# Seven half products instead of eight in five groups of a Trainium2 attention and feed-forward kernel

## The chip, the cores and the metric

One core of one Trainium2 chip runs the kernel. The metric is the time of one execution on the device in microseconds, as a median of several runs. The engines named below are TensorE (PE; its weight loads are PEld), VectorE (DVE), ScalarE (ACT), GpSimd (POOL) and SyncE (SP, which here issues DMAs). Each has its own queue and works it off in order.

## The reference

Attention with normalised queries and keys, and then a gated feed-forward block on its output:

```python
batch, n_heads, seq, head_dim = (8, 12, 448, 64)
q_n, k_n = rmsnorm(q, g_q), rmsnorm(k, g_k)
scores = 1.0 / np.sqrt(64) * np.matmul(q_n, k_n.transpose(0, 1, 3, 2))
attn = np.exp(scores - np.max(scores, axis=-1, keepdims=True))
attn = attn / (np.sum(attn, axis=-1, keepdims=True) + 1e-09)
out = np.matmul(attn, v)
x = out.transpose(0, 2, 1, 3).reshape(8 * 448, 768)
g = x @ w_gate                    # 768 x 1536
val = x @ w_val                   # 768 x 1536
y = (g * (1.0 / (1.0 + np.exp(-g))) * val) @ w_out    # 1536 x 768
```

The attention inputs are float32, the three weights come as float64 and are turned into float32 by the kernel.

## The kernel before

The kernel takes the batches two at a time: four **blocks** of 2 x 448 tokens. Block n has an up phase (`w_gate` and `w_val`, silu and the product of the two), and then a down phase (`w_out`), into which the attention of the next block's 12 pairs of heads is woven. Attention of the first block stands ahead of everything, and the weights are converted beside it and in block 1.

The feed-forward products are made by a bilinear scheme: the two batches of a block and three row thirds of a weight give 6 pieces, a weight has 3 x 3 blocks, and 15 products (numbered 0 to 14) take the place of 18. `UP_ORDER` is the order of the 15. Their left sides, sums of weight blocks, are made once and lie in device memory (`up_sides`, `down_sides`); their right sides, sums of activations, lie in `xs`. `sides` makes them.

An up phase has four **groups** g (0 to 3) of 128 x 3 hidden units. In a group each of the 15 products is made twice, for `w_gate` (`which` 0, banks `mm0` and `mm1`) and for `w_val` (`which` 1, the two banks of `at`), each as two matmuls of 128 x 128 by 128 x 448 (`NC2` halves of the contraction). This is `up_product`, a function within `block`. Products of one chain add up in a PSUM bank, and after each one the bank is read: by ScalarE where the value is new (`COPY`), else by VectorE, which adds to or subtracts from an accumulator. When a result (one of 6 in a group) is complete for the gate, ScalarE applies silu into a PSUM tile `st` (two buffers), and VectorE weighs it by the value: `weigh`. The 24 results of a block lie in `gt`; `combine` makes of them the right sides of the 15 down products, in `hs`, `xs` and `gt`.

Weights come from device memory into two buffers `ws` by `up_load` and `load_sides`: a piece holds five of the 15 products, is issued by SP in two DMAs, and a buffer is free when its last product is done.

The order of instructions on each engine isn't written out. Every piece of work is put into an `Order` with an engine, an estimated duration, a due time (`when`), what it comes after and which buffers it takes or uses; `Order.run` plays this through and emits the pieces in the order that comes out. The due times come from `block_start`, `block_end` and `PRODUCT`, the time of an up product of one `which`.

Of the kernel before, what the change touches and what calls it, by code (L numbers as in the profile page):

```python
# [9 lines left out]
F32 = mybir.dt.float32  # L10
# [350 lines left out]
def transfer(rows, size):  # L361
    return rows * (6.64 + 0.045 * min(size, 4096)) / 16000.0
# [131 lines left out]
def fast(  # L494
# [41 lines left out]
    nc = tc.nc  # L536
# [31 lines left out]
        rr=4, ws=2, **{x + str(i): 1 for x in "vw" for i in range(6)},  # L568
# [14 lines left out]
    OFTEN = dict(w1=0, w2=1, w3=2, w4=3, rows=4)  # L583
# [49 lines left out]
    UP_SUMS = (8, 1, 7, 13, 10, 14, 3, 5, 11, 0, 4)  # L633
# [4 lines left out]
    down_sides = dram.tile([P, 2, NG, 15, P], F32, name="down_sides")  # L638

# [26 lines left out]
    UP, DOWN, BOTH = 30 * NG * PRODUCT, 90.7, 170.0  # L666
# [3 lines left out]

    def block_start(n):
        return FIRST + n * (UP + BOTH) + MORE * (n > 0)

    def block_end(n):
        return block_start(n) + UP + MORE * (n == 0)
# [722 lines left out]
    }  # L1398
    DOWN_READ = {
# [39 lines left out]
    def block(n):  # L1439
        add = order.add  # L1440
        start = block_start(n)
        unit = (block_end(n) - start) / (30 * NG)
# [10 lines left out]
        def up_product(g, step, x, which, load, key):  # L1453
            nonlocal last
            when = start + (2 * (15 * g + step) + which) * unit

            b = ("BCDAE".index(CHAIN[x]) % 2 if CHAIN[x] != "E" else 0) ^ (g % 2) ^ (n > 0)
# [111 lines left out]
        def up_load(g, piece):  # L1569
            key = ("ws", (n, g, piece))  # L1570
            load = add(
                "SP", 1.2, start + (30 * g + 10 * piece) * unit - 24.0,
# [7 lines left out]

        for g in range(NG):
            steps = [(step, which) for step in range(15) for which in range(2)]
            if n == 0 and g == 0:
                steps[: 2 * HEAD] = sorted(steps[: 2 * HEAD], key=lambda of: of[::-1])
            for step, which in steps:
                if step % 5 == 0 and which == 0:
                    key, load = up_load(g, step // 5)
                up_product(g, step, UP_ORDER[step], which, load, key)
        up_done[n] = last
        if n < NB - 1:  # L1590
# [3 lines left out]
            )  # L1594
        bank_read[:] = [free[0, 0], free[0, 1]]
# [32 lines left out]
        for g in range(NG):  # L1628
            when = start + 30 * (g + 1) * unit + 1.0
            before = [down_done.get(n - 1)] + ([staged[HS]] if n == 0 else [])  # L1630
# [8 lines left out]
        def down_product(step, x, s):  # L1639
# [18 lines left out]
            def emit():  # L1658
# [3 lines left out]
                for g in range(NG):  # L1662
                    nc.tensor.matmul(  # L1663
                        banks[s][:, 0:S], w[:, s, g, at], where[x][:, g],
# [6 lines left out]
                    last, loads[piece], bank_read[s], *made.get(x, []),  # L1671
# [10 lines left out]
            def emit_read():  # L1682
# [5 lines left out]
                read(how, tiles[value], old, banks[s][:, 0:S])  # L1688
# [6 lines left out]
            bank_read[s] = drained[s, t] = done  # L1695
# [167 lines left out]
```

## Time and profile before

| what | value |
|---|---|
| time, median of 3 runs | 1454.96 us (1453.89 to 1457.8) |
| span of the profiled execution, first to last instruction | 1452.0 us |
| its own time beyond the span | not recorded; the three runs lie 1.9 to 5.8 us above the span, the median 2.96 |
| mean granted TensorE clock | 0.997 |
| up phase of block 2 (n = 1) | 479.6 to 660.0 us |
| group 0 of block 3 (n = 2) | 826.9 to 872.0 us |
| groups 1 and 2 of block 3 | 872.0 to 962.2 us |
| group 0 of block 4 (n = 3) | 1173.8 to 1218.9 us |
| groups 1 to 3 of block 4 | 1218.9 to 1354.2 us |
| down phase of block 4 | 1354.2 to 1430 us |

The profile is one execution as the hardware profiler saw it. A row of a group of instructions gives line, engine, operation, tiles and shapes, count, busy time, the mean duration in ns, and the idle time of the engine ahead of them with what ended it. A row of the timeline gives start, duration and how many like instructions follow each other. A float32 matmul stands as two instructions, called passes below; a matmul's end is modelled, so consecutive ones overlap in the records and the distance of their starts is what counts.

### The profile page before, as it was taken

Reading aid. Unit: us, or ns where it says so; the run is one execution under the profiler, and the core shown is the slowest. Engines: PE = TensorE matmul, PEld = TensorE weight load, DVE = VectorE, ACT = ScalarE, POOL = GpSimd, SP = SyncE. Lnnn points to the kernel's source line nnn. Section 1 sums busy time; section 2 is a strip of 40 time slices with the busy share of each in tenths; the row PEclk is TensorE's granted clock in tenths of the full one; section 3 lists DMA queues with packets and bytes.
Section 4 is the critical chain, followed back from the end, with each engine's and each line's share of the span. In section 5 each row is a group of like instructions: output and inputs, shape, how many; then the busy total and the mean of one; then the engine's idle time right before and its main releaser. Section 6 shows DMA issues by size and latency. Waiting matters only on the chain.

```text
span 1452.0 us, 19362 instructions
## 1 busy us (share of the span) xinstructions
PE 1426.0 (98%) x6736; PEld 689.5 (47%) x6736; DVE 879.8 (61%) x1485; ACT 601.6 (41%) x1210; POOL 405.7 (28%) x476
## 2 busy tenths in 40 slices
PE   8999999999999999999999999999999999999997
PEld 4455454534444455544444455544444445555553
DVE  5889876878866434546877642455686644442533
ACT  6875444476653222356564122345555322212100
POOL 4756666625443000022443200011434300000000
PEclk9999999999999999999999999999999999999999
DMA  7778979854643533433644623443463452322235
GB/s 196 217 219 268 352 266 310 260 149 90 129 103 64 133 102 92 114 113 70 122 98 86 138 74 107 107 112 93 85 126 77 95 135 73 108 73 90 69 100 110
DMA packets 410416, 193.29 MB, mean 133 GB/s; under 512 B 280004, under 2 KB 390852, under 8 KB 410308
## 3 DMA queue, kind: packets, MB, share of 16 engines
q1 hardware_dynamic: 399040, 190.57, 49.1%
q10 hardware_dynamic: 11140, 1.38, 0.7%
q8 instruction: 55, 0.90, 0.3%
q14 instruction: 53, 0.43, 0.1%
q0 software_dynamic: 128, 0.00, 0.0%
HBM read 157.29 MB, written 34.60 MB: 132 GB/s over the span
## 4 chain that ended last, share of the span: by engine, by line
PE 90%; DMA 3%; DVE 2%; ACT 2%; SPq 1%; issue 1%; POOL 1%; ACTq 0%; DVEq 0%; POOLq 0%
PE at L1474 25%; PE mm L1474 25%; PE mm L1663 23%; PE at L1049 8%; PE st L970 7%; PE st L1080 1%; PE mm L1080 1%; DMA out_dram<-spare 1%; SPq L768 1%; DMA work<-in_k_dram 1%; ACT es L985 1%; DMA xs<-in_moe_w_gate_dram 0%; PE st L908 0%; DMA v<-in_v_dram 0%; ACT work L918 0%
## 5 line engine op out<-in xcount | busy, mean ns | idle before, releaser
L1474 PE MATMUL at<-xs,ws 128*128 128x448 f32 x960 | 401.2, 540 | 2.5 <-DVE v L1413 1.4
L1474 PE MATMUL mm<-xs,ws 128*128 128x448 f32 x960 | 401.7, 541 | 0.2 <-DVE hs L1315 0.2
L1474 PEld LDWEIGHTS at<-xs,ws 128*128 128x128 f32 x960 | 181.4, 190 | 184.7 <-issue 166.7
L1474 PEld LDWEIGHTS mm<-xs,ws 128*128 128x128 f32 x960 | 182.2, 190 | 180.7 <-issue 177.9
L888 POOL TENSOR_TENSOR work<-work,rr 128x448 f32<-128x448 f32 x72 | 71.8, 1016 | 467.5 <-DVE rr L715 341.6
L1663 PE MATMUL mm<-gt,ws 128*128 128x448 f32 x448 | 175.5, 543 | 0.0
L970 PE MATMUL st<-work 64*64 64x448 f32 (+1 forms) x1536 | 151.2, 501 | 10.3 <-ACT work L918 4.9
L985 ACT ACTIVATE es<-st 128x896 f32<-128x896 f32 x129 | 114.2, 914 | 101.6 <-PE at L1049 87.8
L1411 DVE TENSOR_TENSOR gt<-gt,mm 128x448 f32<-128x448 f32 x64 | 39.7, 621 | 188.1 <-PE mm L1474 161.7
L1663 PE MATMUL mm<-hs,ws 128*128 128x448 f32 x384 | 151.3, 544 | 0.0
L990 POOL TENSOR_TENSOR sums<-es 128x896 f32<-128x896 f32 x36 | 77.2, 2145 | 176.8 <-PE st L1080 83.7
L1663 PEld LDWEIGHTS mm<-gt,ws 128*128 128x128 f32 x448 | 83.6, 190 | 83.0 <-issue 80.8
L1551 ACT ACTIVATE st<-gt 128x448 f32<-128x448 f32 x96 | 52.3, 547 | 159.1 <-DVE gt L1415 85.7
L1409 ACT COPY gt<-mm 128x448 f32<-128x448 f32 x80 | 42.6, 532 | 157.5 <-PE mm L1474 157.4
L1049 PE MATMUL at<-es,v 64*64 64x448 f32 (+1 forms) x1032 | 106.0, 507 | 0.0
L1663 PEld LDWEIGHTS mm<-hs,ws 128*128 128x128 f32 x384 | 71.3, 190 | 71.0 <-issue 70.1
L970 PEld LDWEIGHTS st<-work 64*64 64x64 f32 x1536 | 50.9, 133 | 79.1 <-issue 37.4
L1409 ACT COPY v<-at 128x448 f32<-128x448 f32 x96 | 51.0, 532 | 80.4 <-PE at L1474 79.6
L990 POOL TENSOR_TENSOR sums<-sums,es 128x896 f32<-128x896 f32 x36 | 76.0, 2112 | 2.8
L1049 PEld LDWEIGHTS at<-es,v 64*64 64x64 f32 (+1 forms) x1032 | 44.1, 134 | 56.2 <-issue 50.4
L1554 DVE SCALAR_TENSOR_TENSOR gt<-st,v 128x448 f32<-128x448 f32 x96 | 59.7, 622 | 7.3 <-DVE v L1415 0.5
L1411 DVE TENSOR_TENSOR v<-v,at 128x448 f32<-128x448 f32 x64 | 39.8, 621 | 39.6 <-PE at L1474 39.5
(170 smaller groups left out, 1550.5 us busy)
## 6 DMA issues: line engine op xcount, KB each, us to landing
ws<-up_sides SPq DMA_DIRECT2D x32, 1024.0 KB, 5.6
ws<-down_sides SPq DMA_DIRECT2D x16, 1024.0 KB, 5.7
ws<-down_sides SPq DMA_DIRECT2D x28, 512.0 KB, 4.8
ws<-up_sides SPq DMA_DIRECT2D x16, 768.0 KB, 4.9
out_dram<-spare SPq DMA_DIRECT2D x168, 56.0 KB, 2.1
v<-in_v_dram SPq DMA_DIRECT2D x96, 96.0 KB, 2.5
ws<-up_sides SPq DMA_DIRECT2D x32, 256.0 KB, 5.9
ws<-up_sides SPq DMA_DIRECT2D x16, 512.0 KB, 5.8
```

What stands on the lines that cost most here:

```text
L888: nc.gpsimd.tensor_tensor(out=tiles["t", m][:, x], in0=tiles["qk", (m, x)], in1=rr.to_broadcast([P, NC, C]), op=ALU.mult,)
L970: nc.tensor.matmul(st[ds(D * x, D), h, 0:n], tiles["KT", m][rows, ds(P * j + D * of_keys, D)], tiles["QT", m][rows, ds(Q * of_queries, n)] ...
L985: nc.scalar.activation(e, tiles["st", (m, j)][:, :, 0 : S * width(j) // P], AF.Exp)
L990: nc.gpsimd.tensor_tensor(out=to, in0=tiles["e", (m, 0)] if j == 1 else to, in1=e, op=ALU.add)
L1049: nc.tensor.matmul(tiles["at", (m, x)][ds(D * h, D), ds(0, Q) if early else queries], tiles["v", m][rows, j, h], tiles["e", (m, j)][rows, ...
L1080: nc.tensor.matmul(to[ds(D * h + C * x, C)], halves[:, x] if half else many[:, 0:C], term[:, h, 0:Q] if half else term[:, h, ts(x, Q)], st ...
L1409: nc.scalar.copy(to, ps)
L1411: nc.vector.tensor_tensor(out=to, in0=old, in1=ps, op=ALU.add)
L1474: nc.tensor.matmul(ps(), w[:, which, c, at], xs[:, SLOT[x], c], start=fresh and c == 0, stop=c == NC2 - 1, skip_group_check=True,)
L1551: nc.scalar.activation(take(*act, [P, 2, TB])[:, 0, 0:S], to, AF.Silu)
L1554: nc.vector.scalar_tensor_tensor(to, tiles[act][:, 0, 0:S], 1.0 / SCALE, tiles[ready], op0=ALU.mult, op1=ALU.mult,)
L1663: nc.tensor.matmul(banks[s][:, 0:S], w[:, s, g, at], where[x][:, g], start=fresh and g == 0, stop=g == NG - 1, skip_group_check=True,)
```

## The change

In groups 1 and 2 of block 3 and groups 1 to 3 of block 4 (`SEVEN`), the products of a group for one of the 15 are seen as a 2 x 2 by 2 x 2 product of halves: gate and value, the two halves of the contraction (`NC2`), the two halves of the 448 tokens. Eight half products, 224 columns wide, are replaced by seven, with sums ahead and behind:

- **Sums of weights.** `prepare`, in block 2's up phase, reads `up_sides` for groups 1 to 3 in 15 pieces of three products, makes four differences of each on GpSimd (128 x 384 each), and writes the seven left sides to new tensors `up7` in device memory. Its buffers are `es` and parts of `work` that attention uses otherwise.
- **Sums of activations.** `halves_of`, in group 0 of blocks 3 and 4, makes four of each of the 15 right sides on GpSimd (128 x 224 each): S1 in `hs`, S2 in `work`, S4 in `es`, S3 over a part of `xs`, which `restore` puts back ahead of group 3 of block 3.
- **Products.** `sevens` makes four streams X, Y, Z and W for each group. X, Y and Z have two half products for each of the 15, side by side in one bank; W has one. X and Z use the `mm` banks, Y and W those of `at`. In a group of 30 units the streams begin at units 0, 6, 15 and 21 and take a unit for each of the 15, so that two run side by side, and W of one group beside X of the next. In the last group W takes 0.6 units.
- **Sums of results.** When X, Y have a result, GpSimd makes three more sums of it (`combine7`) and one of X alone; its sums (`sow`) go into the accumulators of Z and W ahead of their last reads, in part on VectorE.
- **Loads.** A piece holds three products of X, Y or Z (384 KB), or six of W. The two `ws` buffers are split into six slots `wp`; pieces that begin in the last ten units (`closing`) use slots 3 to 5 alone.
- `combine` waits for Y's last product of the block (`hs_free`). The planner's time of such a group (`SHORT`) is 40.0 instead of 30 x 1.504. `UP_SUMS` is put into another order, and the banks of the down phase are swapped where group 3 has seven products.

```diff
+    SEVEN = {2: (1, 2), 3: (1, 2, 3)}
+    HALF = S // 2
+    up7 = {
+        g: dram.tile([P, 5, 7, 3, P], F32, name=f"up7_{g}")
+        for g in sorted({g for gs in SEVEN.values() for g in gs})
+    }
...
+    PREPARE, PREPARE_PACE, up7_done = {1: [(g, u) for g in (1, 2, 3) for u in range(5)]}, 8.2, {}
...
+        def halves_of():
+            for step, x in enumerate(UP_ORDER):
+                before = [old_done[x], *side_done[n, x], down_done.get(n - 1), clusters[EARLY * (n + 1) - 1, "total"]]
+                for i, (to, one, two, op) in enumerate((
+                    ("S3", "A11", "A21", ALU.subtract), ("S2", "A22", "S3", ALU.subtract),
+                    ("S1", "S2", "A11", ALU.add), ("S4", "A12", "S2", ALU.subtract),
+                )):
+                    done = order.add(
+                        "POOL", 0.55, begin[seven[0] - 1] + (2 * step + 2) * unit + 0.6 * i,
...
+        PARTS = dict(
+            X=((0, "A11"), (1, "S2")), Y=((1, "S1"), (0, "S3")),
+            Z=((0, "A12"), (1, "A22")), W=((0, "S4"),),
+        )
+        SEEN = dict(X=0.0, Y=6.0, Z=15.0, W=21.0)
...
+                for stream in "XYZW":
+                    pace = 0.6 if stream == "W" and g == seven[-1] else 1.0
+                    for i in range(15):
+                        steps.append((begin[g] + (SEEN[stream] + pace * i) * u, stream, g, i))
...
+            until = [begin[seven[0]] - 30.0] * 3 + [begin[seven[0]]] * 3
+            for (stream, g, u), times in sorted(pieces.items(), key=lambda of: of[1][0]):
+                closing = times[0] > begin[seven[-1]] + 20.0 * (begin[seven[-1] + 1] - begin[seven[-1]]) / 30
+                at = min(range(3 if closing else 0, 6), key=lambda at: until[at])
+                key, tile_of = (f"wp{at}", (n, stream, g, u)), ws_keys[at // 3]
...
+                    for side, (_, of) in enumerate(PARTS[stream]):
+                        nc.tensor.matmul(
+                            half(ps(), side), w[side], part_of(of, x),
+                            start=fresh and side == 0, stop=True, skip_group_check=True,
+                        )
...
+                    seeds[g, "U2", result] = combine7(("X", t, 1), ("X", t, 1), ("X", t, 0), when + 1.2, [done], [kx])
+                elif stream == "Y":
+                    u4 = combine7(("Y", t, 0), ("X", t, 1), ("Y", t, 0), when + 1.2, [done, seeds[g, "U2", result]], [kx, ky])
+                    u3 = combine7(("X", t, 1), ("X", t, 1), ("Y", t, 1), when + 1.8, [u4], [kx, ky])
+                    seeds[g, "W2", result] = combine7(("Y", t, 1), ("Y", t, 0), ("Y", t, 1), when + 2.4, [u3], [ky])
...
+                    gated = order.add(
+                        "ACT", 0.55, when - 0.5, gate, after=[acc["gate", g, result]], takes=[act], mode="silu",
+                    )
+                    hidden[g, result] = order.add(
+                        "DVE", 0.62, when + 1.0, weigh, after=[gated, done, seeds[g, "W2", result]], uses=[act, ky],
+                    )
...
+                for i, (to, one, two) in enumerate(((5, 4, 0), (1, 6, 5), (4, 6, 4), (3, 2, 1))):
+                    done = order.add(
+                        "POOL", 0.92, when + 8.0 + i,
+                        lambda raw=raw, to=to, one=one, two=two: nc.gpsimd.tensor_tensor(
+                            out=raw[:, to], in0=raw[:, one], in1=raw[:, two], op=ALU.subtract
+                        ),
...
-            before = [down_done.get(n - 1)] + ([staged[HS]] if n == 0 else [])
+            before = [hs_free, down_done.get(n - 1)] + ([staged[HS]] if n == 0 else [])
```

On SP, at the end of block 4's up phase, this stands before (`ws` are weight buffers, numbered by use; a wait for PE is for a buffer's last product):

```order
L1428 DMA ws_8143<-up_sides3_86 128x4x384 [waits DMAHW4_49,DMAHW3_49,PE_49]
L1428 DMA ws_8143<-up_sides3_86 128x4x256
L1428 DMA ws_8181<-up_sides3_86 128x4x512 [waits DMAHW6_49,DMAHW5_49,PE_49]
L1428 DMA ws_8181<-up_sides3_86 128x4x128
L1428 DMA ws_8220<-down_sides_87 128x8x128 [waits DMAHW7_49,DMAHW0_49,PE_49]
L1428 DMA ws_8220<-down_sides_87 128x8x128
```

At the same place the changed kernel has the pieces W 1, Z 3, Z 4, W 2, Z 5 and W 3 of group 3, and then the first down weights:

```order
L1689 DMA ws_8363<-up7_3_90 128x2x384 [waits DMAHW0_49,PE_49]
L1689 DMA ws_8363<-up7_3_90 128x768 [waits DMAHW1_49,PE_49]
L1689 DMA ws_8363<-up7_3_90 128x768 [waits DMAHW5_49,DMAHW2_49,PE_49]
L1689 DMA ws_8363<-up7_3_90 128x2x384 [waits DMAHW6_49,DMAHW4_49,PE_49]
L1689 DMA ws_8363<-up7_3_90 128x768 [waits DMAHW7_49,DMAHW3_49,PE_49]
L1689 DMA ws_8363<-up7_3_90 128x384 [waits DMAHW5_49,PE_49]
L1444 DMA ws_9091<-down_sides_87 128x8x128 x2
```

Six smaller pieces share one buffer, each waits for PE, and the down weights, which wait for nothing of their own, stand behind them.

PE takes these pieces in the following rows of the changed kernel, from the first that reads Z 3 (waits DMAHW4) by way of Z 4 (DMAHW5) to the first that reads W 2 (DMAHW6); `es` marks W, two rows or x2 are the two halves of Z:

```order
L1737 MATMUL mm0_95<-xs_82,ws_8363 128x224 [waits DMAHW4_49,DVE_49]
L1737 MATMUL mm0_95<-xs_82,ws_8363 128x224
L1737 MATMUL at_97<-es_93,ws_8363 128x224 [waits DVE_49]
L1737 MATMUL mm1_96<-xs_82,ws_8363 128x224 [waits DVE_49]
L1737 MATMUL mm1_96<-xs_82,ws_8363 128x224
L1737 MATMUL at_97<-es_93,ws_8363 128x224 [waits Activation_49] x2
L1737 MATMUL mm0_95<-xs_82,ws_8363 128x224 x2
L1737 MATMUL at_97<-es_93,ws_8363 128x224 [waits Activation_49]
L1737 MATMUL at_97<-es_93,ws_8363 128x224
L1737 MATMUL mm1_96<-xs_82,ws_8363 128x224 [waits DMAHW5_49,DVE_49]
L1737 MATMUL mm1_96<-xs_82,ws_8363 128x224
L1737 MATMUL at_97<-es_93,ws_8363 128x224 [waits DMAHW6_49,DVE_49]
```

Where one matmul of 448 columns with weights of five products stood, a short one now follows the landing of a piece every few products; W 2 takes the slot that Z 3 has left two W and one Z product earlier.

On VectorE, at the end of block 4's up phase, this stands before (L1413 and L1415 read a bank, L1554 weighs, L1185 and L1189 of 128 x 448 are the down phase's first sums for group 3):

```order
L1185 SCALAR_TENSOR_TENSOR hs_89<-gt_88 128x448 [waits DVE_49]
L1415 TENSOR_TENSOR v3_8166<-at_94,v3_8166 128x448 [waits PE_49]
L1554 SCALAR_TENSOR_TENSOR gt_88<-st_8248,v3_8166 128x448 [waits DVE_49,Activation_49]
L1415 TENSOR_TENSOR gt_88<-mm0_92,w0_8214 128x448 [waits PE_49]
L1189 TENSOR_TENSOR hs_89<-gt_88,hs_89 128x448 [waits DVE_49]
L1415 TENSOR_TENSOR v4_8261<-at_94,v5_8218 128x448 [waits PE_49]
L1554 SCALAR_TENSOR_TENSOR gt_88<-st_8258,v4_8261 128x448 [waits DVE_49,Activation_49]
L1413 TENSOR_TENSOR gt_88<-gt_88,mm1_93 128x448 [waits PE_49]
L1413 TENSOR_TENSOR v1_8152<-v1_8152,at_94 128x448 [waits PE_49]
L1554 SCALAR_TENSOR_TENSOR gt_88<-st_8269,v1_8152 128x448 [waits DVE_49,Activation_49]
```

And this after (L1429 reads a bank, L1804 is a sum for Z or W, L1891 weighs, L1200 is the first of the down phase's sums):

```order
L1429 TENSOR_TENSOR gt_91<-gt_91,mm0_95 128x448 [waits PE_49]
L1804 TENSOR_TENSOR spare_81<-spare_81 128x224 [waits DVE_49]
L1429 TENSOR_TENSOR spare_81<-spare_81,at_97 128x224 [waits PE_49]
L1891 SCALAR_TENSOR_TENSOR gt_91<-st_9044,spare_81 128x448
L1891 SCALAR_TENSOR_TENSOR gt_91<-st_9078,spare_81 128x448 [waits Activation_49]
L1891 SCALAR_TENSOR_TENSOR gt_91<-st_9105,spare_81 128x448 [waits Activation_49]
L1891 SCALAR_TENSOR_TENSOR gt_91<-st_9108,spare_81 128x448 [waits Activation_49]
L1891 SCALAR_TENSOR_TENSOR gt_91<-st_9111,spare_81 128x448 [waits Activation_49]
L1891 SCALAR_TENSOR_TENSOR gt_91<-st_9116,spare_81 128x448 [waits Activation_49]
L1200 SCALAR_TENSOR_TENSOR hs_92<-gt_91 128x448 [waits DVE_49]
```

The weighings, which stood between the reads, all follow the last read, and the down phase's first sum for group 3 follows them. Of the first down product on PE the fourth matmul, that of group 3, waits for VectorE.

More of the change, by code (lines that the diff above doesn't have):

```diff
@@ L1588, in block @@
                 up_product(g, step, UP_ORDER[step], which, load, key)
+                old_done[UP_ORDER[step]] = last
+            if seven and g == seven[0] - 1:
+                halves_of()
+        if n in PREPARE:
+            prepare()
         up_done[n] = last
```

312 lines of the change are left out of this document (297 added, 15 removed).

## The prediction

> **What bounds the kernel now.** I read the page first: busy time, then the chain that ended last.
>
> ```profile
> PE 1426.0 (98%) x6736; PEld 689.5 (47%) x6736; DVE 879.8 (61%) x1485; ACT 601.6 (41%) x1210; POOL 405.7 (28%) x476
> PE 90%; DMA 3%; DVE 2%; ACT 2%; SPq 1%; issue 1%; POOL 1%; ACTq 0%; DVEq 0%; POOLq 0%
> ```
>
> TensorE is busy for 98% of the span and is 90% of the chain. Then the windows of the stretches that change, columns PE, PEld, DVE, ACT, POOL, clock, DMA share, GB/s: block 2's up phase; groups 1 and 2 of block 3; groups 1 to 3 of block 4.
>
> ```profile
> 479.60:660.00 180.40, 180.40 (x516) 89.93 (x515) 77.48 (x138) 62.89 (x120) 11.94 (x10) 1.00 0.39 105
> 872.00:962.20 90.20, 90.20 (x241) 45.60 (x240) 37.78 (x64) 25.76 (x50) 1.84 (x2) 1.00 0.43 109
> 1218.90:1354.20 135.30, 135.30 (x361) 68.40 (x360) 51.54 (x84) 29.02 (x54) 0.00 (x0) 1.00 0.27 86
> ```
>
> PE has no gap in any of them; a group takes 135.3 / 3 = 45.1 us. So PE time taken out there comes out of the span, unless PE then waits for something new.
>
> **What the change removes.** A group is 60 matmuls of 448 columns, and the last row's 361 instructions on PE are two passes for each. After, it is 105 matmuls of 224 columns: 120 passes become 210. No row shows a 128x128 pass of 224 columns, so I bound it by a wider and a narrower one.
>
> ```profile
> 1352.72 1.67 PE L1474 MATMUL at<-xs,ws 128*128 128x448 f32 x4
> L1474 PE MATMUL at<-xs,ws 128*128 128x448 f32 x960 | 401.2, 540 | 2.5 <-DVE v L1413 1.4 <-ACT v L1409 0.6 <-DVE v L1415 0.3
> L1474 PEld LDWEIGHTS at<-xs,ws 128*128 128x128 f32 x960 | 181.4, 190 | 184.7 <-issue 166.7 <-DVE v L1411 5.7 <-DVE v L1413 5.0
> 9.50 0.93 PE L908 MATMUL st<-ident,work 112*128 112x112 f32 x8
> L908 PE MATMUL st<-ident,work 112*128 112x112 f32 x96 | 12.0, 265 | 2.1 <-POOL work L881 1.1 <-ACT es L985 0.8 <-ACT more L985 0.2
> L908 PEld LDWEIGHTS st<-ident,work 112*128 112x128 f32 x96 | 9.4, 140 | 10.0 <-POOL work L881 5.7 <-issue 3.1 <-POOL xs L1339 1.2
> ```
>
> Passes of 448 columns start every (1.67 - 0.54) / 3 = 0.377 us; the window of block 4 gives 135.3 / 360 = 0.376. Transposes of 112 columns, each with its own load of 128 columns, start every (0.93 - 0.265) / 7 = 0.095 us, so a load of that width does not hold passes back even there. The line through both gives 0.189 us at 224 columns (half of 0.376 is 0.188). A group is then 210 x 0.189 = 39.7 us: 5.4 us less, five times: **-27.0 us**.
>
> **What it adds: waits for weights where the streams close.** Today each piece of weights is issued one piece ahead:
>
> ```profile
> 872.01 1.67 PE L1474 MATMUL mm<-xs,ws 128*128 128x448 f32 x4
> 872.21 1.19 SPq L1428 DMA_DIRECT2D ws<-up_sides  x2
> ws<-up_sides SPq DMA_DIRECT2D x32, 1024.0 KB, 5.6
> ws<-down_sides SPq DMA_DIRECT2D x28, 512.0 KB, 4.8
> work<-in_q_dram SPq DMA_DIRECT2D x12, 224.0 KB, 3.9
> v<-in_v_dram SPq DMA_DIRECT2D x96, 96.0 KB, 2.5
> up_sides<-hs SPq DMA_DIRECT2D x4, 960.0 KB, 5.4
> ```
>
> SP issues 0.20 us after the buffer's last product has streamed and the data are wanted 15 us later; landing takes 5.6. With the change six slots serve the streams, and I counted, in the order of PE, the products between a slot's last use and its next piece's first. In the middle of the streams these are 7.6 us and more, at an opening 5.3. But the last six pieces of block 3's group 2 and of block 4's group 3 share three slots (`closing`). There Z's third piece has one Z and one W product between (0.756 + 0.378 = 1.13 us), W's second 1.51, W's third 2.65; the other three 4.2 to 4.5. The pieces are 384 KB, W's third 192. Landing is bounded by 2.5 us (96 KB) and 4.8 (512 KB, a neighbour in flight); the line from 96 to 960 KB gives 3.5 and 2.8, which I take. With the 0.20 the waits are 3.7 - 1.13 = 2.6, 3.7 - 1.51 = 2.2 and 3.0 - 2.65 = 0.35: 5.1 a closing, **+10.2 us** for two. By the bounds a closing costs 2.8 to 9.3 (at 4.8 W's first piece waits too).
>
> SP works in order, so block 3's first weights of group 3 stand behind W's third piece, though their buffer is free. That piece is issued 0.2 us after its slot's last product, 4.9 us before the streams end with their waits; 0.6 later the 1024 KB go out and land 5.6 after: 0.2 + 0.6 + 5.6 - 4.9 = **+1.5 us** (0 to 2.5). In block 4 the down weights come as late, but hide behind the next term.
>
> **The end of block 4.** Today weighing stands between the reads, and the down phase starts without a gap. In the new VectorE order all six weighings of group 3 come after the very last read, then the sum for down product 6, whose fourth matmul waits for it.
>
> ```profile
> 1352.92 0.62 DVE L1413 TENSOR_TENSOR gt<-gt,mm 128x448 f32<-128x448 f32 x1
> 1354.22 4.30 PE L1663 MATMUL mm<-hs,ws 128*128 128x448 f32 x11
> L1189 DVE TENSOR_TENSOR hs<-hs,gt 128x1792 f32<-128x1792 f32 x8 | 16.1, 2015 | 4.1 <-PE mm L1663 4.0
> L1411 DVE TENSOR_TENSOR v<-v,at 128x448 f32<-128x448 f32 x64 | 39.8, 621 | 39.6 <-PE at L1474 39.5
> L1554 DVE SCALAR_TENSOR_TENSOR gt<-st,v 128x448 f32<-128x448 f32 x96 | 59.7, 622 | 7.3 <-DVE v L1415 0.5
> L1551 ACT ACTIVATE st<-gt 128x448 f32<-128x448 f32 x96 | 52.3, 547 | 159.1 <-DVE gt L1415 85.7 <-DVE gt L1413 33.1 <-DVE gt L1528 23.5
> L1185 DVE SCALAR_TENSOR_TENSOR hs<-gt 128x448 f32<-128x448 f32 x16 | 9.9, 617 | 0.0
> ```
>
> A read begins 0.20 us after its product has streamed (1352.92 against 1352.72). From the last product's end T: VectorE is still at Z's last read (T - 0.18 to T + 0.44), then a W sum and the last W read, 224 columns each, 0.39 by the line from 448 to 1792 columns: T + 1.22. Six weighings of 0.622, each pair also bound by silu (two buffers, 0.547 + 0.622), are 3.75: T + 5.0; the sum ends at T + 5.6. Three matmuls go ahead (6 x 0.376 = 2.25): **+3.4 us** (2 to 5). In block 3 the same tail falls beside group 3's products, and VectorE is busy there for less than half the time (37.78 of 90.20 us in the window above).
>
> **Small terms.** At the two openings X runs alone on two banks for six steps: a read by VectorE returns its bank 0.20 + 0.62 us after the product, the other bank's product lasts 0.756; **+0.6** (0 to 2). GpSimd's sums stand ahead of reads of Z and W:
>
> ```profile
> L1336 POOL TENSOR_TENSOR es<-es 128x128 f32<-128x128 f32 x20 | 8.6, 455 | 0.3
> L1339 POOL TENSOR_TENSOR es<-es 128x256 f32<-128x256 f32 x8 | 5.8, 728 | 10.9 <-DVE es L1315 8.8 <-PE at L1474 1.8
> L990 POOL TENSOR_TENSOR sums<-sums,es 128x896 f32<-128x896 f32 x36 | 76.0, 2112 | 2.8
> 123.60:303.00 179.40, 174.75 (x480) 85.97 (x481) 140.06 (x215) 84.47 (x126) 117.14 (x221) 0.99 0.89 290
> ```
>
> Two plain operands cost 0.66 us at 224 columns and 1.14 at 448 on these rows' line, 23 us of a group's 39.7. From Y's tenth step five results bring three sums each: 9.9 us against 7.6 of PE. The backlog ends some 5.4 us after Y, and the tightest of the sums that Z's reads need ends at 7.7, when PE has its product at 7.6: **+0.5** in all (0 to 6). Block 2's 60 differences (1.0 us each at 384 columns, in 123 us) and block 3's and 4's 60 halves (40 us beside 45 of group 0) meet an idle GpSimd. Block 1's up phase, last row, is the cover: GpSimd busy 117 us, DMA at 0.89, and PE still 97%. I take 0 (up to 2 if it goes). Block 2's transfers add 2.1 MB per 8.2 us, about 260 GB/s, to weights with 9 us to spare. At 0 too.
>
> **The sum.** -27.0 + 10.2 + 1.5 + 3.4 + 0.6 + 0.5 = **-10.8 us**: the span of 1452.0 becomes 1441.2. The runs have a median of 1454.96, 2.96 around that span, which I keep: **1444.2 us**.
>
> **Rivals.**
> *The weights are in time.* The closings cost only what the lower bound leaves or less, the others as above: -27 + 5 = -22, 1433. For it: a closing stretch moves few bytes. Against: 1.13 us is below even the 2.5 of a 96 KB load. 0.12.
>
> *GpSimd and VectorE hold each other up in every group.*
>
> ```profile
> 301.88 2.34 POOL L990 TENSOR_TENSOR sums<-es 128x896 f32<-128x896 f32 x1 [3.72 <-ACT es L985]
> 302.14 2.56 DVE L1528 TENSOR_TENSOR gt<-gt,w 128x448 f32<-128x448 f32 x1
> ```
>
> A sum of VectorE on two operands in SBUF took 2.56 us, not 0.62, beside a GpSimd sum. The change gives a group eight such VectorE sums and 32 on GpSimd; half a GpSimd sum lost each time is about 4 us of VectorE. It has slack (30 PSUM-wide operations of 0.62 for X, Y and Z, 12 of 0.39 for W, two sums and six weighings are 28 us of 39.7), so I charge PE 2 us a group: +10, to 1454. Against: the reads themselves come from PSUM, and slow sums are few in that row's group. 0.15. The Trainium skill, "GPSIMD Engine Reference", 1. Specifications, says the same of VectorE instructions with two SBUF inputs; the 2.56 us agrees.
>
> *Slower: a small piece takes as long as today's large one.* Place: the closings. If 384 KB take the 5.6 us of the 1024 KB row, the four waits there are 4.7, 4.3, 2.7 and 1.3, with Z's later pieces near 1.5 each: some 15 a closing. -27 + 30 + 5 = +8, 1463. It turns slower where a load exceeds about 5.3 us, since each microsecond more costs three waits in each of two closings. For: 256 KB loads of the weights land in 5.9. Against: those are issued right behind 1024 KB. 0.08.
>
> *The weight load is not hidden.* If each of the 90 added passes of a group showed its 0.190 us load, five groups would lose 85 us: about 1530. The 0.095 us of the transposes speaks against it: 0.03. The Trainium skill, "TensorE: Matmul & The Clock Gate", Part 3, The mechanism, says that a weight load overlaps matmuls in flight only where the row group differs, which here it never does. By that rule this rival would hold; the transposes' row disagrees.
>
> **Chances.** Forecast 0.62 (1436 to 1452 by the bounds of its terms, the upper ones not all at once), then 0.12, 0.15, 0.08, 0.03. Faster by over 0.3% (below 1450.6; about what a measurement here can tell from no change): nearly all of the forecast, the first rival, a third of the second: 0.75. Within: 0.14. Slower: 0.11. The range reaches to the first two rivals: 1433 to 1454.
>
> **What would show it.** Passes of 224 columns starting 0.189 us apart; in each closing three PE gaps of 2.6, 2.2 and 0.4 us ended by DMA of weights; 1.5 us ahead of block 3's group 3; 3.4 us inside the first down product of block 4, ended by VectorE. It is wrong if passes are further apart, if the gaps stand in the middle of groups and are ended by VectorE or GpSimd, or if block 2 loses PE time.

## The result, and the profile after

| | before | after |
|---|---|---|
| time, median of 4 runs each on one chip | 1455.13 us (1453.89 to 1457.8) | 1516.53 us (1513.29 to 1517.27) |
| ratio, 95% interval | 1 | 1.0411 (1.0395 to 1.0426) |
| span of the profiled execution | 1452.0 us | 1511.4 us |
| mean granted TensorE clock | 0.997 | 0.987 |

The kernel became 4.1% slower; the forecast was 1444.2 us, faster. These are busy time after the change, and below it the chain that ended last, by engine:

```profile
PE 1434.3 (95%) x7186; PEld 767.1 (51%) x7186; DVE 939.3 (62%) x1605; ACT 621.0 (41%) x1266; POOL 671.5 (44%) x831
PE 73%; DMA 10%; SPq 5%; DVE 4%; POOL 3%; ACT 3%; issue 1%; DVEq 0%; ACTq 0%; POOLq 0%
```

TensorE has fallen from 98% to 95% of a longer span and from 90% to 73% of the chain; DMA, SP, VectorE and GpSimd have come in. TensorE's busy time itself has hardly grown (1426.0 to 1434.3 us), so most of what was added is waits. The first instruction of each stretch, read from TensorE's timeline in both traces, says where:

| stretch | before, us | after, us | difference | forecast |
|---|---|---|---|---|
| start of block 2's up phase | 479.6 | 480.7 | +1.1 | 0 |
| from there to block 3's up phase | 347.3 | 374.3 | **+27.0** | 0 |
| from there to block 4's up phase | 346.9 | 361.8 | **+14.9** | -3.7 |
| block 4's up phase | 180.4 | 193.8 | **+13.4** | -10.5 |
| the rest | 97.8 | 100.8 | +3.0 | +3.4 |
| sum | | | +59.4 | -10.8 |

The forecast column splits the prediction's terms by place. Nearly half the loss lies between the starts of block 2's and block 3's up phases, where no product is formed differently and only the weights are prepared. The windows after, columns PE, PEld, DVE, ACT, POOL, clock, DMA share and GB/s: block 2's up phase, groups 1 and 2 of block 3, groups 1 to 3 of block 4.

```profile
480.73:660.46 179.73, 161.03 (x426) 79.15 (x424) 63.71 (x109) 43.13 (x85) 62.71 (x64) 0.94 0.83 272
900.15:1002.08 101.93, 91.11 (x421) 76.35 (x420) 54.81 (x98) 28.26 (x59) 58.93 (x83) 0.98 0.53 151
1261.99:1410.65 148.66, 135.38 (x632) 113.65 (x631) 84.55 (x150) 41.35 (x86) 72.89 (x100) 0.99 0.45 139
```

Block 2 has gaps of 18.7 us and a clock of 0.94, where before it had none and 1.00. A group of halves takes 101.93 / 2 = 51 us and 148.66 / 3 = 49.6, against 45.1 before and 39.7 forecast for its passes alone.

**Block 2.** TensorE's waits there, then SP's between 480 and 640 us (columns: us in total, times, longest), and two of the page's DMA rows (KB each, us to landing):

```profile
PE mm L1492 <- DMA ws<-up_sides: 12.5, 4, 6.8
PE at L1492 <- ACT v L1425: 6.2, 1, 6.2
```
```profile
SPq L1926 <- DMA up<-work: 47.1, 6, 9.0
SPq L1926 <- DMA up<-es: 25.6, 6, 6.0
```
```profile
up<-es SPq DMA_DIRECT2D x8, 1344.0 KB, 7.4
up<-work SPq DMA_DIRECT2D x7, 1344.0 KB, 8.0
```

Line 1926 is `prepare`'s load. Before it may overwrite a buffer, the store out of that buffer must have landed, which takes a median of 7.4 to 8.0 us; SP stands at twelve of these loads, 72.7 us in all, and TensorE's weights (line 1444) wait their turn on SP behind them. SP's and TensorE's timelines around the two longest gaps show it:

```profile
602.47 1.21 SPq L1926 DMA_DIRECT2D work<-up_sides  x2
603.72 2.50 SPq L783 DMA_DIRECT2D work<-in_q_dram  x4
606.32 0.77 SPq L1946 DMA_DIRECT2D up<-es  x1
607.14 1.96 SPq L1444 DMA_DIRECT2D ws<-up_sides  x2
609.14 6.44 SPq L783 DMA_DIRECT2D work<-in_k_dram  x4
615.69 1.56 SPq L1926 DMA_DIRECT2D es<-up_sides  x2
617.35 0.56 SPq L1946 DMA_DIRECT2D up<-work  x1
```
```profile
616.20 3.36 PE L1492 MATMUL mm<-xs,ws 128*128 128x448 f32 x4 [6.85 <-DMA ws<-up_sides]
625.72 3.35 PE L1492 MATMUL at<-xs,ws 128*128 128x448 f32 x4 [6.16 <-ACT v L1425]
```

SP gets past line 1926 only at 602.47, when the store issued at 593.54 has landed, and issues the weights at 607.14, behind loads of q and a store. They land 9 us later at 616.2: a gap of 6.85. The next gap, 6.16, ends with a read by ScalarE that came late. Four passes then take 3.36 us where they took 1.67: the granted clock is 0.50 from 611.9 to 629.0 us.

**The groups of halves.** The spacing of the starts of their 1,050 passes, from TensorE's timeline: 834 of 1,048 follow the one before by less than 0.25 us, nearly all by 0.189. Against 0.189 for each, they add 52.1 us in all:

| distance to the pass before | passes | above 0.189 in all |
|---|---|---|
| 0.25 to 0.45 us, around 0.293 and 0.377 | 181 | 22.3 us |
| over 0.45 us (a gap) | 33 | 28.8 us |
| less than 0.25 us | 834 | 1.0 us |

Of the 181, 153 write to `at`. The rows of the passes by tile (count, busy us, mean ns, idle before) show it too: products on `mm` have a mean of 352 to 361, and so have those on `at` that stand second in their product (`at<-xs`); the ones that stand first (`at<-hs`, `at<-es`) are slower.

```profile
L1737 PE MATMUL mm<-xs,ws 128*128 128x224 f32 x450 | 113.0, 361 | 6.6 <-DVE hs L1200 2.4 <-DMA ws<-up 2.3 <-ACT v L1425 1.1
L1737 PE MATMUL at<-hs,ws 128*128 128x224 f32 x150 | 47.9, 401 | 4.4 <-DVE spare L1427 3.6
L1737 PE MATMUL at<-es,ws 128*128 128x224 f32 x150 | 44.5, 385 | 13.1 <-DVE more L1427 4.6 <-DMA ws<-up 3.9 <-DVE spare L1431 2.1
L1737 PE MATMUL at<-xs,ws 128*128 128x224 f32 x150 | 40.6, 352 | 0.0
```

A piece of the timeline of that time, ScalarE's and TensorE's rows (PE, and PEld its weight loads):

```profile
1326.33 0.54 PE L1737 MATMUL at<-xs,ws 128*128 128x224 f32 x2
...
1326.90 0.53 ACT L1425 COPY spare<-at 128x448 f32<-128x448 f32 x1 [4.66 <-PE at L1737]
1327.08 0.54 PE L1737 MATMUL mm<-work,ws 128*128 128x224 f32 x2
1327.49 0.30 PEld L1737 LDWEIGHTS at<-hs,ws 128*128 128x128 f32 x2 [0.21 <-ACT spare L1425]
1327.49 0.65 PE L1737 MATMUL at<-hs,ws 128*128 128x224 f32 x2
```

ScalarE reads the Y product of 1326 until 1327.43, and at 1327.49 the next Y product starts, though it goes to the other bank. In the code `at` is one tensor with two banks, `mm0` and `mm1` are two tensors. The theory, tested below, is that a write to `at` therefore waits for the last read of `at`, whichever bank that was in.

**The closings.** In block 3: 2.35, then 1.99 us; in block 4 2.33 and 1.91, the latter two shown here (the profile names DMA for them and for block 3's second), with the gap inside the first down product:

```profile
1391.45 0.99 PE L1737 MATMUL mm<-xs,ws 128*128 128x224 f32 x4 [2.33 <-DMA ws<-up]
1399.25 0.62 PE L1737 MATMUL at<-es,ws 128*128 128x224 f32 x2 [1.91 <-DMA ws<-up]
1415.82 4.40 PE L2046 MATMUL mm<-hs,ws 128*128 128x448 f32 x11 [2.75 <-DVE hs L1200]
```

### The profile page after: what moved, and what is told of

The parts are those of the page before. It is cut to its first block, busy times and chain, and to the rows that moved or that the text cites. A ratio compares the mean times of both kernels' runs of the same rounds, so it can differ in the third digit from the quotient of the medians.

```text
span 1511.4 us, 21173 instructions
## 1 busy us (share of the span) xinstructions
PE 1434.3 (95%) x7186; PEld 767.1 (51%) x7186; DVE 939.3 (62%) x1605; ACT 621.0 (41%) x1266; POOL 671.5 (44%) x831
## 4 chain that ended last, share of the span: by engine, by line
PE 73%; DMA 10%; SPq 5%; DVE 4%; POOL 3%; ACT 3%; issue 1%; DVEq 0%; ACTq 0%; POOLq 0%
PE mm L2046 23%; PE at L1492 12%; PE mm L1492 11%; PE at L1064 7%; PE st L985 7%; PE at L1737 5%; PE mm L1737 5%; DMA up<-es 3%; DMA up<-work 3%; SPq L783 2%; PE st L1095 1%; SPq L1926 1%; DMA work<-in_k_dram 1%; PE mm L1095 1%; ACT es L1000 1%
## 5 line engine op out<-in xcount | busy, mean ns | idle before, releaser
L1492 PE MATMUL mm<-xs,ws 128*128 128x448 f32 x660 | 279.5, 547 | 12.7 <-DMA ws<-up_sides 12.5
L1492 PE MATMUL at<-xs,ws 128*128 128x448 f32 x660 | 279.1, 546 | 11.6 <-ACT v L1425 8.7
L1492 PEld LDWEIGHTS mm<-xs,ws 128*128 128x128 f32 x660 | 126.0, 192 | 139.7 <-issue 122.3
L1492 PEld LDWEIGHTS at<-xs,ws 128*128 128x128 f32 x660 | 125.3, 192 | 140.9 <-issue 114.3
L903 POOL TENSOR_TENSOR work<-work,rr 128x448 f32<-128x448 f32 x72 | 72.7, 1027 | 221.1 <-DVE rr L730 142.8
L1737 PE MATMUL mm<-xs,ws 128*128 128x224 f32 x450 | 113.0, 361 | 6.6 <-DVE hs L1200 2.4
L1737 PEld LDWEIGHTS mm<-xs,ws 128*128 128x128 f32 x450 | 85.2, 193 | 12.5 <-DVE hs L1200 5.3
L1569 ACT ACTIVATE st<-gt 128x448 f32<-128x448 f32 x66 | 36.1, 547 | 102.3 <-DVE gt L1431 56.0
L822 ACT ACTIVATE work<-work 128x448 f32<-128x448 f32 (+1 forms) x92 | 52.1, 585 | 39.2 <-DMA v<-in_v_dram 16.3
```

Source lines behind the costliest of these rows:

```text
L822: nc.scalar.activation(tiles["t", m][:, x], of, AF.Square)
L903: nc.gpsimd.tensor_tensor(out=tiles["t", m][:, x], in0=tiles["qk", (m, x)], in1=rr.to_broadcast([P, NC, C]), op=ALU.mult,)
L1492: nc.tensor.matmul(ps(), w[:, which, c, at], xs[:, SLOT[x], c], start=fresh and c == 0, stop=c == NC2 - 1, skip_group_check=True,)
L1569: nc.scalar.activation(take(*act, [P, 2, TB])[:, 0, 0:S], to, AF.Silu)
L1737: nc.tensor.matmul(half(ps(), side), w[side], part_of(of, x), start=fresh and side == 0, stop=True, skip_group_check=True,)
```

## The experiments

Each variant but the last was run once. On one chip, fifteen runs of the kernel before lie between 1452.71 and 1458.07 us, so a difference of a few microseconds between single runs is read from the traces and not from the times. Where code is shown in part, `...` stands for the lines between or behind.

**First set of runs.** Theory 1: block 2 loses its 27 us because SP stands at `prepare`'s loads. Theory 2: the groups lose because `at` is one tensor. Rivals: both losses are GpSimd's or DMA's load, or the closings.

*The preparation alone.* Block 2 prepares all weights, and blocks 3 and 4 form eight products as before, so the prepared weights are never read.

```diff
-        return sum(SHORT if i in SEVEN.get(n, ()) else 30 * PRODUCT for i in range(g))
+        return sum(30 * PRODUCT for i in range(g))
...
-        seven = SEVEN.get(n, ())
+        seven = ()
```

> Block 2 makes the differences and writes them, but every group of blocks 3 and 4 is computed with eight products as before, so the differences are never read. If block 2 loses by this preparation alone, the time is that of before plus the 27 us by which the start of block 3 has moved: about 1482 us, with the same PE gaps ended by DMA of weights between 558 and 630 us. If block 2's loss comes from elsewhere (the new order of the weight sums, the seven products' buffers), it is within 3 us of before, 1455.

Measured: 1480.80 us beside 1456.65 for the kernel before on the same chip, +24.2. Block 2's up phase takes as long as in the changed kernel (212.1 and 212.0 us to the down phase, 185.3 before) and TensorE waits there as it did: 12.5 us in four gaps for `ws<-up_sides`, 6.2 for ScalarE. Blocks 3 and 4 take what they took before. The preparation costs this by itself.

*`at` as two tensors.* The only other use of both banks at once, a multiplication in the attention, is split into two.

```diff
-            tiles[name, key] = at_banks[:, at]
+            tiles[name, key] = at_banks[at]
...
-    at_banks = psum.tile([P, 2, TB], F32, name="at", bufs=1)
+    at_banks = [psum.tile([P, TB], F32, name=f"at{i}", bufs=1) for i in range(2)]
...
```

> The changed kernel, with the two banks of at as two tensors of one bank each instead of one tensor of two (the early attention's division is then two instructions of 224 columns instead of one of 448). If a product of Y or W waits for the read of the Y or W product just before it, in the other bank, only because both banks are one tensor, then the waits of some 0.1 to 0.3 us ahead of most at products go, with the 0.10 us by which the pass after such a wait is late: about 7 us a group, 35 in all, 1481 us. If those waits are set by the sums of GpSimd and the order on VectorE, they stay and the time is within 5 us of 1516.

Measured: 1480.47, 36 us under the changed kernel's median; the spans differ by 32.7 (1511.4 and 1478.7). Two of the rows above, now with the split:

```profile
L1738 PE MATMUL at<-es,ws 128*128 128x224 f32 x150 | 42.5, 374 | 5.7 <-DMA ws<-up 4.0 <-DVE more L1428 1.2 <-DVE spare L1428 0.2
L1738 PE MATMUL at<-hs,ws 128*128 128x224 f32 x150 | 40.6, 352 | 0.0
```

`at<-hs` is down from 401 to 352 ns and waits for nothing. Of the 52.1 us above 0.189 in the groups of halves, 30.0 are left: 55 late passes (7.4 us) in place of 181, 18 gaps (22.2 us) in place of 33. So the shared tensor cost 22.2 us between the passes of the groups. By stretches, up to the first pass behind each, block 1's up phase is 3.4 us shorter, block 2's 5.5, the groups of halves 8.3 and 11.2 (a new gap behind their last pass takes 2.7 of the 22.2 back), group 3 of block 3 2.9 and all the rest 1.5, which is the 32.7 to rounding.

*Six slots in the closings.*

```diff
-                at = min(range(3 if closing else 0, 6), key=lambda at: until[at])
+                at = min(range(6), key=lambda at: until[at])
```

> The changed kernel, with all six slots for the weights of the closing streams instead of three. If the two PE gaps of 2.0 to 2.4 us in each closing come from a slot that is freed too late, they go: 8 to 10 us less, about 1507. If the weights that follow (group 3 of block 3, the down phase of block 4) now come as much later, the gain is under 4 us.

Measured: 1514.90, 1.6 us under the changed kernel's median and within its own range. The waits for `ws<-up` are gone from block 3's closing, and its groups of halves are 2.6 us shorter; but reads by VectorE are waited for longer there, and in block 4 the groups gain 0.7 and the rest is 1.6 longer. Blocks 1 and 2, where the edit changes nothing, are 1.9 and 1.1 us longer in this run, which hides part of the gain. So the slots set the waits for weights in the closings, but the closings are not what cost most of the time, and three slots more move part of the wait to VectorE.

*The preparation's loads and stores on GpSimd's queue* instead of SP's.

```diff
-                            nc.sync.dma_start(
+                            nc.gpsimd.dma_start(
...
-                    lambda raw=raw, g=g, u=u: nc.sync.dma_start(
+                    lambda raw=raw, g=g, u=u: nc.gpsimd.dma_start(
...
```

> The changed kernel, with the loads and stores of the preparation in block 2 issued by GpSimd's queue instead of SP's: the same bytes, the same sums. If block 2 loses because loads of the preparation wait on SP for a store's landing while PE's weights stand behind them, the gaps between 558 and 630 us go: about 25 us less, 1491. If the bandwidth of the transfers sets them, they stay: within 6 us of 1516.

Measured: 1529.26, slower still, and a miss. Its windows show why, columns as above; then a row of ScalarE's timeline:

```profile
480.00:520.00 40.00, 40.00 (x107) 20.16 (x107) 17.20 (x26) 9.86 (x17) 24.36 (x27) 1.00 0.96 317
520.00:560.00 40.00, 40.00 (x108) 20.26 (x107) 13.40 (x22) 8.58 (x16) 23.02 (x27) 1.00 0.77 266
560.00:602.00 42.00, 42.00 (x113) 20.97 (x111) 14.71 (x25) 8.06 (x15) 17.85 (x21) 1.00 0.88 268
602.00:637.00 35.00, 0.13 (x1) 0.00 (x0) 2.31 (x3) 2.62 (x8) 19.24 (x24) 0.57 0.82 276
```
```profile
633.53 1.04 ACT L822 ACTIVATE work<-work 128x448 f32<-128x448 f32 x2 [39.10 <-DMA up<-work]
```

For 122 us the theory holds: with SP free, TensorE has no gap, though the DMA share rises to 0.96 and 317 GB/s. Then it stands for 35 us. ScalarE is at the first squares of the next attention (line 822), which need the buffer of the preparation's last pieces, and waits 39 us until their store has landed; its reads of PSUM stand behind that, and TensorE behind them. The preparation ends too late in both kernels. In the changed one the same place costs the 6.16 us gap above. The profile puts ScalarE's wait there down to a load of v, issued at 617.95; but that load had not landed when the squares began at 624.67, while the store issued at 617.35 had, at 624.57, 7.2 us after its issue.

**Second set of runs.** So two things have to go from block 2: the queue and the length. `SEVEN` with two groups in each of blocks 3 and 4 needs ten pieces instead of fifteen. All runs of this set but the first form fewer groups of halves than the changed kernel.

*The kernel before, with `at` as two tensors.*

> The kernel before, with the PSUM tensor `at` made two tensors of one bank. Theory: the shared tensor costs only where a product's read comes back later than the one product between; with 448 columns that product lasts 1.504 us and hides it nearly always (four late products in block 1 of before, 2.5 us in all), so about 1452, 0 to 4 us under before. Rival: most of the 36 us that the split brought has nothing to do with the products of halves, and before gains as much: about 1420.

Measured: 1451.49 beside 1454.38, as the theory had it. The split is worth 32.7 us of span to the changed kernel; to the old one 2.9 in this pair of runs, and 1.1 in the longer comparison at the end.

*Two groups, SP's queue, a piece every 12 us, `at` as two tensors.*

```diff
-    SEVEN = {2: (1, 2), 3: (1, 2, 3)}
+    SEVEN = {2: (1, 2), 3: (1, 2)}
-    PREPARE, PREPARE_PACE, up7_done = {1: [(g, u) for g in (1, 2, 3) for u in range(5)]}, 8.2, {}
+    PREPARE, PREPARE_PACE, up7_done = {1: [(g, u) for g in (1, 2) for u in range(5)]}, 12.0, {}
```

> The changed kernel with `at` as two tensors, only groups 1 and 2 of blocks 3 and 4 formed of seven products, so ten pieces prepared instead of fifteen, one every 12 us. Theory (the preparation loses time because a piece comes round every 9 us or so with two buffers, while 8.2 are planned, so that SP stands at its loads with PE's weights behind it, and its last pieces reach into the next attention): with 12 us no stall is left, 24 us under the 1480.5 of the run with the split; the third group of block 4 gained nothing there (136.1 against 135.4), so about 1456. Rival (the bytes themselves are too many for the DMA beside the weights): two thirds of the bytes lose two thirds of the time, about 1472.

Measured: 1472.81, the rival's number. The slower pace does not help: SP still stands 48.7 us at eight loads (line 1927 here), and the first 408 passes of block 2's up phase take 163.3 us, 153.6 before.

```profile
SPq L1927 <- DMA up<-work: 30.9, 4, 7.9
SPq L1927 <- DMA up<-es: 17.8, 4, 6.5
```

But the rival's reason, bytes, falls with the next run but one.

*The gates' seed sums on VectorE.*

```diff
-  result, "POOL", when - 4.0, [last_of(stream, t), seeds[g, stream, result]], seed[result],
+  result, "DVE" if stream == "Z" else "POOL", when - 4.0, [last_of(stream, t), seeds[g, stream, result]], seed[result],
```

> The kernel with two groups, and the three sums by which a gate result takes up its seed (U3 into Z) made by VectorE instead of GpSimd. Theory (PE's gap of 2.4 us at each change of group is GpSimd, whose three sums of 1.2 us stand behind 24 sums of halves): two to four gaps of 2.4 us go, 5 to 8 us under the kernel with two groups. Rival (the gap is VectorE's own queue): no change, or 2 to 4 us more.

Measured: 1470.54, 2.3 us under the run before: less than the theory asked, more than the rival, and too little to tell from none in single runs. The gap at the change of group stays (2.26 and 2.25 us), so the theory falls. VectorE now waits itself, for a GpSimd sum of halves, as its timeline in this run shows:

```profile
915.46 0.62 DVE L1805 TENSOR_TENSOR gt<-gt,v 128x448 f32<-128x448 f32 x1 [3.38 <-POOL v L1869]
```

*Two groups, GpSimd's queue, a piece every 10 us, `at` as two tensors.*

> The kernel with two groups, preparing one piece every 10 us, with the preparation's loads and stores issued by GpSimd's queue. Theory (the 35 us stall of the run with GpSimd's queue was ScalarE standing at an attention square for the buffer of the last pieces, not the queue): ten pieces are done some 30 us before that square, so within 3 us of the kernel with two groups, about 1456. Rival (issuing on GpSimd costs by itself): over 1470.

Measured: 1461.93, 10.9 us under the run with SP's queue. Windows: block 2's up phase, and groups 1 and 2 of block 3.

```profile
478.20:632.00 153.80, 153.80 (x417) 77.64 (x419) 68.00 (x115) 47.37 (x94) 64.04 (x71) 1.00 0.78 243
870.91:963.72 92.81, 84.35 (x421) 79.41 (x419) 55.92 (x98) 28.57 (x59) 59.32 (x83) 0.98 0.58 166
```

Block 2 is as it was before the change: TensorE full, clock 1.00. The same ten pieces in the same bytes, faster paced, cost nothing once no load of theirs stands ahead of TensorE's weights, and once they end before the attention wants their buffers. The Trainium skill, "DMA: Bandwidth & Descriptors", Issuing engines are not separate DMA queues, says that issuing from several engines saves only the time of issuing, usually small. Here it saved the 9.7 us by which block 2's up phase was longer on SP's queue, since an engine that issues a load also stands at that load's wait (SP's 48.7 us in the run before). What is left against the kernel before (+7.5 us) lies in the groups: 92.8 and 94.0 us for two, where eight products took 90.2, and 1.5 us in block 4 until the next group's weights land.

**Third set of runs**, from that last kernel.

*Six of GpSimd's sums later*, so that the ones that the gates wait for come first.

```diff
-                    seeds[g, "W2", result] = combine7(("Y", t, 1), ("Y", t, 0), ("Y", t, 1), when + 2.4, [u3], [ky])
+                    seeds[g, "W2", result] = combine7(("Y", t, 1), ("Y", t, 0), ("Y", t, 1), when + 8.0, [u3], [ky])
```

> The kernel with two groups, two tensors and GpSimd's queue (1461.9), with the six W2 sums of a group due 8 us after their product instead of 2.4, so that GpSimd makes the U3 sums, which the gates wait for, first. Theory (the 2.4 us gap at the change of group is the length of GpSimd's row of sums): six sums of 0.7 us leave that row, the two gaps shrink from 2.4 to under 0.7 us, about 1458. Rival (the row is set by when its results arrive, or VectorE is as late): gaps stay over 2 us, 1461 to 1463.

Measured: 1460.08, but both gaps are the same 2.40 us, so the theory falls and the rival stands. VectorE's row ahead of it, and GpSimd's that it waits for:

```profile
909.55 1.16 DVE L1432 TENSOR_TENSOR gt<-mm,gt 128x448 f32<-128x448 f32 x2 [2.42 <-POOL gt L1805]
```
```profile
907.77 0.66 POOL L1805 TENSOR_TENSOR spare<-spare 128x224 f32<-128x224 f32 x1
908.38 1.13 POOL L1805 TENSOR_TENSOR gt<-gt,v 128x448 f32<-128x448 f32 x1
```

TensorE waits for VectorE, VectorE for GpSimd, and GpSimd works without a pause from 899.9 to 910.7. That GpSimd is late at the change of a group is shown; which of its sums would have to go was not found by these two edits.

*W's last products spread out.*

```diff
-  pace = 0.6 if stream == "W" and g == seven[-1] else 1.0
+  pace = 0.9 if stream == "W" and g == seven[-1] else 1.0
```

> As the run with later sums, and the W products of a block's last group of halves spread over 0.9 of a product's time each instead of 0.6, so that their last ones lie among the next group's products. Theory (the two gaps of 2.0 to 2.3 us in each closing are weights that cannot be fetched because three slots are all in use while nothing else is left to multiply): the next group's products cover them, 4 to 8 us less, 1450 to 1454. Rival (the slots come free later still, so that the next group's first weights come later): no gain, 1458 to 1462.

Measured: 1461.03, the rival: in each closing two weight gaps of 2.0 to 2.3 us stay.

*The kernel with two groups and GpSimd's queue, `at` as one tensor again.*

> The kernel with two groups and GpSimd's queue (1461.9), with `at` one tensor of two banks again, as in the changed kernel. Theory (the shared tensor costs about 4.5 us in each group of halves, and 3 to 4 us in block 1, whatever the preparation does): 20 to 26 us more, 1482 to 1488. Rival (part of the 36 us was the split easing the preparation): 1470 to 1478.

Measured: 1486.17, 24.2 us more than with two tensors, as the theory had it. Its 838 distances stand 44.6 us above 0.189 in all, against 27.8 with the split. Block 2's up phase differs by only 0.3 us here, so the price of the shared tensor in groups and in block 1 doesn't hang on the preparation.

*The kernel before with `at` as two tensors, in five rounds.*

> The kernel before with `at` as two tensors, timed in five rounds. Theory (four late products of block 1 and their openings, 3.4 us of PE's row, and nothing else): 1451 to 1452, ratio 0.997 to 0.9985. Rival (the single look was chance): 1454 to 1456.

Measured: 1453.24 against 1454.33, ratio 0.9989 (0.998 to 0.9998): between the theory and the rival, a gain of a tenth of a per cent whose interval only just leaves out none. In the trace block 1's first 408 passes do take 3.4 us less (156.9 and 153.5). No version with products of halves came under the kernel before. Whether a third `ws` buffer would take the closings' waits away was not tried.

## Why the prediction was wrong, point by point

- **"Block 2's transfers add 2.1 MB per 8.2 us, about 260 GB/s, to weights with 9 us to spare. At 0 too."** This step failed, by 27.0 us (26.0 over the same stretch of the run with the preparation alone, whose time was 24.2 longer). It weighed bandwidth, and rightly: 317 GB/s went through without a gap in the run with GpSimd's queue. The prediction used "SP works in order" for the closings, but not here. So it left out two waits that the change itself adds: a load into a buffer waits on SP until the buffer's store has landed, with TensorE's weights behind it, and the attention waits for the buffers of the last pieces. The cycle of a buffer was never worked out; SP alone waited 72.7 us for it. The prediction named the sign ("if block 2 loses PE time") but made no rival of it.
- **"210 x 0.189 = 39.7 us".** The spacing is right: 0.189 us for four passes in five, with the 0.190 us weight load hidden. The lost part is what stands between: 52.1 us in five groups, of which the forecast had the 10.2 of the closings and about 1 of small terms.
- **"X runs alone on two banks"** in the small terms. This is the second step that failed: for Y and W the two banks of `at` act as one, since they are one tensor. With one product of 0.756 us between two of `at`, a read that returns its bank 0.20 + 0.53 to 0.62 us after the product is just too late, with some 0.06 us from the read's end to the product's start (1327.43 to 1327.49 above); before, 1.504 us lay between, and hid it nearly always. This cost 22.2 us between the passes of the groups, 32.7 over the span with what it delays elsewhere.
- **The closings.** Of the waits of 2.6, 2.2 and 0.35, the two large ones came as 2.35 and 1.99, 2.33 and 1.91, with 384 KB landing in 3.3 us (3.5 taken). For these two the mechanism and size were right, and with six slots they are gone from block 3's closing. At the place of the third stands a wait of 0.85 us for VectorE. The rivals on either side, "the weights are in time" and 5.6 us for a small piece, are out.
- **Group 3 of block 3** (+1.5): the time was longer by 3.4 us, but not for this reason. Ahead of its second product for `w_val` there is a gap of 1.89 us, ended by ScalarE's read, not by weights, and it goes with the split. With the split there is 1.1 us ended by `up_sides`, near the forecast.
- **The end of block 4** (+3.4): 2.75 us inside the first down product, ended by VectorE's `hs`, as told.
- **GpSimd and VectorE.** The +0.5 was too low. GpSimd's estimates held (0.66 us at 224 columns, 1.13 at 448), but the backlog that this term names ends later than was taken: 2.4 us of TensorE at three changes of group once the shared tensor is gone (1.5 us stand there in the changed kernel, ended by VectorE's reads of `at`). The rival put 2 us a group on sums that VectorE makes slowly beside GpSimd. Two such sums in block 3's groups do take 1.05 us in the mean (line 1852), but what VectorE waits for ahead of these gaps is GpSimd's row, so the rival was near in size by another cause.
- **Weight load not hidden** is out as a rule for every pass. It is seen only behind a wait, in the last section.

In the run with two groups, GpSimd's queue and the split, a group of halves still takes about 46.7 us against 45.1: passes 39.7, and 7 us of waits and late passes. There the saving of 5.4 us in a group is smaller than what the waits around seven products cost. Which part of the 7 us could still be removed stays open.

## What to carry to other kernels

When a step brings its own loads and stores, work out a buffer's full cycle (load, work, store landed) and who stands behind it on the queue that issues it, before counting bytes; then ask who wants the buffer last. When the work between two uses of a resource is halved, look again at every wait that was hidden by a narrow margin: whether two banks are two tensors to the program, and whether a read comes back within the new, shorter time. Set a saving of a few microseconds in each group beside the waits that its ends can bring: here 5.4 us beside 7.

## What the runs showed of the hardware that was not expected

- In these rows the pass behind a wait loads its weights only when the wait is over: at 1327.49 the load is recorded at the pass's own start, where the next products' loads start 0.19 us ahead of their passes. The pair of passes has records that reach over 0.65 us where its neighbours' reach over 0.54, and its second pass follows at 0.293 instead of 0.189, 0.104 us later. It is there with wide passes too. In the kernel before, a run of four behind a gap is 0.10 us longer than its neighbours:

```profile
170.30 1.67 PE L1474 MATMUL mm<-xs,ws 128*128 128x448 f32 x4
172.96 1.77 PE L1474 MATMUL at<-xs,ws 128*128 128x448 f32 x4 [1.00 <-DVE v L1413]
```

  So waits of 0.03 us (the one at 1327.49) and of 1.00 us both cost 0.10 us on top. In the groups the 181 late passes, which are late by such waits or behind them, add 22.3 us. The Trainium skill, "TensorE: Matmul & The Clock Gate", in its table of specifications, says that TensorE's queue pulls weight loads ahead of matmuls in flight. The 0.189 us spacing agrees; that a wait in front of the product stops it is what these rows add.
- Behind the gaps of 6.85 and 6.16 us two runs of four passes took 3.36 and 3.35 us instead of 1.67, so these gaps cost 3.4 us more at a granted clock of one half. Behind the gap of 2.95 us that ended at 576.75 the granted clock was 0.5 for 3.4 us as well.
- Where the preparation ran, TensorE's weights, 1024 KB, took 9.2 us to land (the trace's DMA issues between 480 and 640 us, median of six) instead of the 5.6 of before:

```profile
ws<-up_sides SPq DMA_DIRECT2D x6, 1024.0 KB, 9.2
```
